# The bonus of eight chunks summed on TensorE instead of GpSimd, with the opening put in another order

## The chip, the core and the metric
The kernel runs on one core of one Trainium2 chip. The metric is the time of one execution on the device in microseconds (us), the median of several runs; lower is better. PE is TensorE, DVE is VectorE, ACT is ScalarE, POOL is GpSimd, and SP is the engine that issues the loads.

## What is computed
A recurrence over 768 time steps for 4 batches of 8 heads of 48 elements, and a gated feed-forward network (FFN) on its output.

```
for t in range(768):                                     # per batch and head
    y[t]  = r[t] @ (state + outer(u * k[t], v[t]))       # u * k: the "bonus" of the step itself
    state = w[t][:, None] * state + outer(k[t], v[t])
x = y as 3072 rows of 384 = 8 * 48
out = (sigmoid(x @ w_gate) * (x @ w_val)) @ w_out        # 384 -> 1536 -> 384
```

The bonus part of y[t] is the number sum(r[t] * u * k[t]) of each head, times v[t].

## The kernel before, in words
The steps are cut into 24 chunks of 128 (6 along time for each of 4 batches; c0 to c3 are the first chunks of the four batches, c4 to c7 the second). Of each chunk two tensors are loaded. `pin` holds decay, k and r "in lanes": 112 partitions (two heads of 48 at 0 and 64), four pairs of heads along the free axis. `tok` holds r, k and v "in rows": 128 time steps by 3 x 384. A chunk passes through

- `prep_k`, `prep_r` (DVE): two scans over the decay (L320, L337), k and r multiplied by them (L326, L342);
- `turn_k` (PE, four transposes, L352), `take_k` (ACT copy), `sums` (PE), `middle` and `keep` (the state after half a chunk and at its end);
- `scores` (PE), `mask` (DVE, two), `mix` (PE), `take_y` (DVE, two: adds the bonus), `turn_x` (PE), `take_x` and `rest_x` (ACT and DVE split x into a high and a low part);
- the bonus: `bonus1`, `bonus2` (POOL: r*u, then *k, in rows), `bonus3` (DVE: sum over each head, L309), `bonus4` (POOL: times v, L313).

The FFN's 12 weights w0 to w11 come as 64-bit floats, 1152 KB each. DVE rebuilds 32-bit floats from the words in three instructions (L250, L254, L258), ACT rounds off a high part (L263), DVE subtracts the low part (L266). ACT also checks each weight's range (`w_guard`). One FFN unit is one weight for one group of rows: `gate` and `value` on PE (pg and pu, nine matmuls each, L450), sigmoid, product, high and low part on ACT and DVE (sg, hm, hh, hl; L461 to L476), and `down` on PE (po, three matmuls a chunk, L485).

The first two rounds of four chunks (n = 0, 1) are cut into two groups of two chunks each. Their units, the chunks c0 to c12 and the weights are put in order at build time by `Plan`: each step has an engine, a guessed cost, the steps that it needs, the buffers that it takes and gives (`ROOM`), and a rank. `TURNS` gives the rank of chunks and weights, `COMES` the order of the loads on SP (strictly in order), `LAGS` how far the four FFN groups are set back. The later rounds are written out in a fixed loop. Each engine then works through its instructions in order; SP too, so a load that waits for a buffer holds all loads behind it. `pin` and `tok` have two buffers each.

Of the kernel before, what the change touches and what calls it, by code (L numbers as in the profile page):

```python
# [32 lines left out]
TURNS = "c0 w0 c1 w1 c2 w2 w3 w4 w5 c3 w6 w7 w8 c4 w9 w10 w11 c5 c6 c7 c8 c9 c10 c11 c12"  # L33
COMES = "p0 t0 ub w0 p1 p2 t1 w1 w2 p3 t2 t3 w3 w4 w5 t4 p4 w6 w7 w8 w9 w10 w11 p5 t5 t6 p6 t7 p7 p8 t8 t9 p9 p10 p11 t10 t11 p12 p13 t12 t13"
GROUPS = [(0, 0, 2), (0, 2, 4), (1, 0, 2), (1, 2, 4)]
LAGS = [0, 6.5, 15, 16]
ROOM = dict(pin=2, tok=2, bon=2, eg=1, ready=2, mid=2, kT=1, at=1, bank=2, x=2, full=1, pg=1, pu=1, unit=4, po0=1, po1=1, po2=1, po3=1)
HC = C // 2
HALVES = [slice(0, HC), slice(HC, C)]
HW = 3 * DM // 2  # L40
# [100 lines left out]
class Plan:  # L141
# [5 lines left out]
    def add(self, name, engine, cost, after, rank, work=None, take=(), give=()):  # L147
        self.ops[name] = (engine, cost, [a for a in after if a], rank, work, take, give)

    def run(self):  # L150
        left = {n: set(o[2]) for n, o in self.ops.items()}
        room, free, ends, order, started = self.room, {}, [(0.0, "")], [], set()
        transfers = [n for n in sorted(self.ops, key=lambda n: self.ops[n][3]) if self.ops[n][0] == "SP"]
        while ends:
            now = min(ends)[0]
            for e in [e for e in ends if e[0] <= now]:
                ends.remove(e)
                if e[1] in self.ops:
                    for r in self.ops[e[1]][6]:
                        room[r] += 1  # L160
                    for n in left:
                        left[n].discard(e[1])
            moved = True
            while moved:
                moved = False
                for n in sorted((n for n in self.ops if n not in started and not left[n]), key=lambda n: self.ops[n][3]):
                    engine, cost, _, _, work, take, _ = self.ops[n]
                    if engine and free.get(engine, 0.0) > now or engine == "SP" and n != transfers[0]:
                        continue
                    if any(room[r] < take.count(r) for r in take):  # L170
                        continue
                    for r in take:
                        room[r] -= 1
                    if engine:
# [7 lines left out]
                    if work:  # L182
                        work()
# [477 lines left out]
```

## Time and profile before

| what | us |
|---|---|
| median of 3 runs | 620.96 (620.81 to 621.43) |
| the profiled execution's own time | 622.11 |
| its span in the profile | 620.4 |
| PE busy | 577.6 |
| DVE, ACT, POOL busy | 334.7, 201.5, 96.6 |

The profile lists for one execution what each engine did and when, and what ended each idle time. Busy time of PE counts slow matmuls too: the granted clock says how fast PE was allowed to run, 1.00 at 2.4 GHz, 0.50 at 1.2 GHz. Of a stretch, the difference between its length and PE's busy time is time in which PE stood.

### The profile page before, as it was taken

What the parts mean: (1) busy time and instruction counts of PE and PEld (TensorE: products, weight loads), DVE (VectorE), ACT (ScalarE), POOL (GpSimd) and SP (SyncE); (2) the same over time, 40 slices, a digit from 0 to 9 for tenths busy, and PEclk for the clock granted to TensorE, in tenths of its full rate; (3) what the DMA queues carried; (4) which work ended last, traced back from release to release, by engine and by line L of the source; (5) the groups of instructions that cost most, each with busy time, mean ns of one, the idle gap of its engine ahead of it and who ended that gap; (6) DMA issues with size and microseconds to landing.
All of it is one profiled execution on the core that took longest, in us unless ns stands there. A gap on an engine that the chain in (4) does not pass through costs nothing. (4 is left out here: it accounts for less than half of the span.)

```text
span 620.4 us, 13068 instructions
## 1 busy us (share of the span) xinstructions
PE 577.6 (93%) x5706; PEld 513.6 (83%) x5706; DVE 334.7 (54%) x570; ACT 201.5 (32%) x402; POOL 96.6 (16%) x86
## 2 busy tenths in 40 slices
PE   4477799999999999799999999999999999999994
PEld 3376699999999999688888888888888888888884
DVE  4979879989575743234544544644644544212120
ACT  2638783444323322212312322312322312221112
POOL 3342111111121402002202202202202201000000
PEclk9998899999999999989999999999999999999999
DMA  8687920023223130121022042022042000000001
GB/s 247 232 323 275 348 85 1 2 84 109 76 82 124 46 123 1 52 84 50 35 84 53 33 134 66 18 84 69 17 135 84 1 1 2 25 28 0 1 2 55
DMA packets 12050, 50.76 MB, mean 82 GB/s; under 512 B 1376, under 2 KB 4576, under 8 KB 10448
## 3 DMA queue, kind: packets, MB, share of 16 engines
q1 hardware_dynamic: 8528, 45.11, 22.2%
q10 hardware_dynamic: 3456, 4.72, 2.1%
q8 instruction: 47, 0.77, 0.5%
q14 instruction: 19, 0.16, 0.1%
HBM read 45.11 MB, written 4.72 MB: 80 GB/s over the span
## 5 line engine op out<-in xcount | busy, mean ns | idle before, releaser
L450 PE MATMUL pg<-x,w 128*128 128x256 f32 (+1 forms) x864 | 173.9, 347 | 1.2 <-DVE w L266 1.2
L450 PE MATMUL pu<-x,w 128*128 128x256 f32 (+1 forms) x864 | 171.4, 344 | 0.0
L450 PEld LDWEIGHTS pg<-x,w 128*128 128x128 f32 x864 | 137.9, 193 | 18.0 <-DVE w L266 1.6
L450 PEld LDWEIGHTS pu<-x,w 128*128 128x128 f32 x864 | 136.7, 192 | 17.2
L485 PE MATMUL po<-w,hh 128*128 128x384 f32 x576 | 147.8, 338 | 0.0
L468 DVE TENSOR_TENSOR sg<-pu,sg 128x256 f32<-128x256 f32 (+1 forms) x96 | 53.4, 556 | 151.2 <-PE pu L450 150.1
L485 PE MATMUL po<-w,hl 128*128 128x384 f32 x288 | 101.6, 353 | 7.2 <-DVE hl L476 7.0
L485 PEld LDWEIGHTS po<-w,hh 128*128 128x128 f32 x576 | 105.2, 189 | 0.9
L472 ACT CAST hh<-sg 128x256 fp32r<-128x256 f32 (+1 forms) x96 | 49.1, 512 | 168.9 <-DVE sg L468 168.4
L461 ACT ACTIVATE sg<-pg 128x256 f32<-128x256 f32 (+1 forms) x96 | 46.9, 488 | 158.9 <-PE pg L450 158.1
L313 POOL TENSOR_TENSOR bon<-tok,a 128x384 f32<-128x384 f32 x24 | 35.2, 1465 | 296.9 <-DVE a L309 296.9
L476 DVE TENSOR_TENSOR hl<-sg,hh 128x256 fp32r<-128x256 f32 (+1 forms) x96 | 55.1, 574 | 38.8 <-ACT hh L472 38.8
L485 PEld LDWEIGHTS po<-w,hl 128*128 128x128 f32 x288 | 54.4, 189 | 10.7 <-DVE hl L476 8.7
L302 POOL TENSOR_TENSOR bon<-tok,ub 128x384 f32<-128x384 f32 x24 | 31.9, 1330 | 117.5 <-DMA tok<-tok 51.1
L424 DVE TENSOR_TENSOR bon<-pa,bon 128x192 f32<-128x192 f32 x48 | 15.6, 352 | 42.3 <-PE pa L417 42.3
L347 ACT ACTIVATE junk<-eg 112x1032 bf16<-112x1032 f32 x24 | 25.6, 1066 | 31.2 <-DVE eg L337 31.1
L417 PEld LDWEIGHTS pa<-tok,at 64*64 64x64 f32 x768 | 26.7, 143 | 9.1 <-issue 5.1
L320 DVE TENSOR_TENSOR_SCAN eg<-pin,ends 112x516 f32<-112x516 f32 x24 | 30.0, 1249 | 4.2 <-DMA pin<-dec 4.2
L417 PE MATMUL pa<-tok,at 64*64 64x48 f32 x768 | 29.9, 229 | 2.3 <-DVE at L383 2.3
L383 DVE TENSOR_TENSOR at<-pa,after 128x256 f32<-128x256 f32 x48 | 18.6, 418 | 24.7 <-PE pa L377 24.7
L337 DVE TENSOR_TENSOR_SCAN eg<-pin,heads 112x516 f32<-112x516 f32 x24 | 31.0, 1292 | 0.0
L395 PEld LDWEIGHTS pv<-tok,kT 64*48 64x48 f32 (+1 forms) x704 | 21.0, 137 | 10.7 <-issue 4.7
(58 smaller groups left out, 445.1 us busy)
## 6 DMA issues: line engine op xcount, KB each, us to landing
pin<-dec SPq DMA_DIRECT2D x23, 675.5 KB, 5.1
tok<-tok SPq DMA_DIRECT2D x24, 576.0 KB, 4.3
wraw<-wts SPq DMA_DIRECT2D x12, 1152.0 KB, 12.1
y<-o ACTq DMA_DIRECT2D x24, 192.0 KB, 2.1
pin<-dec SPq DMA_DIRECT2D x1, 448.0 KB, 4.1
pin<-dec SPq DMA_DIRECT2D x1, 227.5 KB, 2.6
ub<-u SPq DMA_DIRECT2D x1, 192.0 KB, 7.4
```

The source lines that it names most:

```text
L302: nc.gpsimd.tensor_tensor(out=bon[q], in0=tk[q][:, 0:DM], in1=ub, op=ALU.mult)
L313: nc.gpsimd.tensor_tensor(out=by_head(bon[q]), in0=by_head(tk[q][:, 2 * DM:]), in1=a0, op=ALU.mult)
L320: nc.vector.tensor_tensor_scan(out=e[:, 516:0:-1], data0=t[:, 516:0:-1], data1=ends[:, 516:0:-1], initial=0.0, op0=ALU.mult, op1=ALU.add,)
L337: nc.vector.tensor_tensor_scan(out=e[:, WW:WW + 516], data0=t[:, 0:516], data1=heads[:, 0:516], initial=0.0, op0=ALU.mult, op1=ALU.add,)
L347: nc.scalar.activation(junk, both, AF.Square, accum_out=acc_d[:, q:q + 1])
L417: nc.tensor.matmul(bank["y", q, o][half, p], lhsT=att[q][half, o, p], rhs=values(q, p, o, half), start=q < B and not s and p == 0, stop=p ...
L450: nc.tensor.matmul(t, lhsT=w[f][:, cols], rhs=x[n][:, a, k, i0 * C:i1 * C], start=k == 0 and j == 0, stop=k == NKT - 1 and j == 2)
L461: nc.scalar.activation(sg, hid["g", n, f, i0], AF.Sigmoid)
L468: nc.vector.tensor_tensor(out=sg, in0=hid["u", n, f, i0], in1=sg, op=ALU.mult)
L472: nc.scalar.copy(hh, hid["s", n, f, i0])
L476: nc.vector.tensor_tensor(out=hl, in0=hid["s", n, f, i0], in1=hid["hi", n, f, i0].bitcast(F32), op=ALU.subtract)
L485: nc.tensor.matmul(po[n, i][:, :DM], lhsT=h[:, c], rhs=w[f][:, 2 * DM:], start=f == 0 and j == 0, stop=f == NFF - 1 and j == 2,)
```

## The change
For the first eight chunks (`FAST`) the bonus takes another way. DVE multiplies r by k in lanes (`product`, before prep_k overwrites k). In `turn_k` four more matmuls, one per pair of heads, take that product as weights and two columns of u (`ul`, zero outside its head) as the moving operand: the sums of the eight heads land behind the transposes, in the same bank, and ACT copies them to `a0`. POOL is left with `bonus4`; `tok` of these chunks loads v only. `ul` is cleared by POOL and loaded by two loads of single elements. `ub`, which only later chunks need, is loaded later.

Beside that: `w_guard` writes its unused result in bf16 to a buffer shared with `guard`; the last four outputs have a buffer each and are copied by ACT and DVE in turn, stored from ACT and SP; the planner's search is rewritten with a heap; costs of PE steps in the first round are set higher; and `TURNS`, `COMES` and `LAGS` are new.

```diff
-COMES = "p0 t0 ub w0 p1 p2 t1 w1 w2 p3 t2 t3 w3 w4 w5 t4 p4 w6 ...
-LAGS = [0, 6.5, 15, 16]
+COMES = "p0 ul t0 p1 w0 p2 t1 w1 t2 w2 p3 t3 w3 w4 w5 w6 p4 w7 t4 ...
+LAGS = [0, 1.5, 19, 14]
...
+FAST = 8
...
     def load_tok(q):
-        nc.sync.dma_start(tk[q], tok[place(q)])
+        first = 2 * DM if q < FAST else 0
+        nc.sync.dma_start(tk[q][:, first:], tok[place(q)][:, first:])
...
+    def load_u():
+        for o in range(2):
+            nc.sync.dma_start(ul[64 * o:64 * o + D, :, o], u.rearrange("(p o d) -> o d p", o=2, d=D)[o])
+    def product(q):
+        rk[q] = p1.tile([L, NP, C], F32, tag="rk", name=f"rk{q}")
+        nc.vector.tensor_tensor(out=rk[q], in0=rr(q), in1=kk(q), op=ALU.mult)
...
     def turn_k(q):
...
+        if q < FAST:
+            for p in range(NP):
+                nc.tensor.matmul(t[:, NP * L + 2 * p:NP * L + 2 * p + 2], lhsT=rk[q][:, p], rhs=ul[:, p], start=True, stop=True)
...
     def take_k(q):
...
+        if q < FAST:
+            bank["a0", q] = p2.tile([P, H], F32, tag="a0", name=f"a0{q}")
+            nc.scalar.copy(bank["a0", q], bank["k", q][:, NP * L:NP * L + H])
...
+    def send(n, i):
+        final = n == NC_ - 1
+        o = p2.tile([P, DM], F32, tag=("o", "tok", "pin", "bon")[i] if final else "o", name=f"o{n}_{i}")
+        rows = out[place(n * B + i) * C:(place(n * B + i) + 1) * C, :]
+        if final and i % 2:
+            nc.vector.tensor_copy(o, po[n, i][:, :DM])
+            nc.sync.dma_start(rows, o)
+        else:
+            nc.scalar.copy(o, po[n, i][:, :DM])
+            nc.scalar.dma_start(rows, o)
```

The order on SP at the start, before (the number behind a name is that of the buffer's use; pin, tok and wraw come in the order of their chunks and weights):

```order
L277 DMA pin_103<-dec 112x520
L278 DMA pin_103<-dec 112x1024
L285 DMA tok_106<-tok 128x1152
L514 DMA ub<-u 128x384
L237 DMA wraw_113<-wts 128x1152
L280 DMA pin_179<-dec 112x1544
L280 DMA pin_205<-dec 112x1544
L285 DMA tok_210<-tok 128x1152
L237 DMA wraw_226<-wts 128x1152
L237 DMA wraw_261<-wts 128x1152
L280 DMA pin_303<-dec 112x1544
```

and now:

```order
L288 DMA pin_105<-dec 112x520
L289 DMA pin_105<-dec 112x1024
L314 DMA ul<-u 48x4x1 x2
L297 DMA tok_110<-tok 128x384
L291 DMA pin_112<-dec 112x1544
L248 DMA wraw_120<-wts 128x1152
L291 DMA pin_219<-dec 112x1544
L297 DMA tok_242<-tok 128x384
L248 DMA wraw_244<-wts 128x1152
L297 DMA tok_262<-tok 128x384
L248 DMA wraw_285<-wts 128x1152
L291 DMA pin_350<-dec 112x1544
```

The load of ul stands ahead of tok0, pin1 ahead of w0; tok of chunk 2 has come between w1 and w2.

On DVE, the stretch up to the second x, which the first FFN unit needs, before (pin_205 is chunk 2, w_220 and w_341 are w0 and w1):

```order
L424 TENSOR_TENSOR bon_229<-pa_1_270,bon_229 128x4x48
L337 SCALAR_TENSOR_TENSOR eg_329<-pin_205,heads 112x516
L342 TENSOR_TENSOR pin_205<-pin_205,eg_329 112x512
L442 TENSOR_TENSOR x_217<-px_345,x_217 128x3x128
L266 TENSOR_TENSOR w_341<-full_296,w_341 128x1152
```

and now (full_347 and w_355 belong to w2, pin_350 is chunk 3):

```order
L265 SCALAR_TENSOR_TENSOR full_347<-wraw_285,full_347 128x1152
L412 TENSOR_TENSOR at_318<-pa_0_319,after 128x256
L269 SCALAR_TENSOR_TENSOR full_347<-wraw_285,full_347 128x1152
L412 TENSOR_TENSOR at_318<-pa_1_320,after 128x256
L277 TENSOR_TENSOR w_355<-full_347,w_355 128x1152
L453 TENSOR_TENSOR bon_250<-pa_0_319,bon_250 128x4x48
L319 TENSOR_TENSOR rk_377<-pin_350 112x512
L453 TENSOR_TENSOR bon_250<-pa_1_320,bon_250 128x4x48
L343 SCALAR_TENSOR_TENSOR eg_382<-pin_350,ends 112x516
L347 RECIPROCAL heads<-eg_382 112x4
L349 TENSOR_TENSOR pin_350<-pin_350,eg_382 112x512
L471 TENSOR_TENSOR x_260<-px_386,x_260 128x3x128
```

Three weights, w0, w1 and w2, are now finished ahead of the second x, where before only w0 was; the k part of chunk 3 has come ahead of it too.

On PE, the end of the planned part (the second round's last units, then the first unit of the fixed loop), before:

```order
L450 MATMUL pg_2_11_3113<-x_1026,w_1586 128x256 x9
L485 MATMUL po_2_2198<-w_1462,hl_2_10_3123 128x384
L485 MATMUL po_2_2198<-w_1462,hh_2_10_3111 128x384 x2
L485 MATMUL po_3_2202<-w_1462,hl_2_10_3123 128x384
L485 MATMUL po_3_2202<-w_1462,hh_2_10_3111 128x384 x2
L450 MATMUL pu_2_11_3133<-x_1026,w_1586 128x256 x9
L485 MATMUL po_2_2198<-w_1586,hl_2_11_3146 128x384
```

and now:

```order
L479 MATMUL pg_0_11_3147<-x_1113,w_1594 128x256 x9
L479 MATMUL pu_0_11_3163<-x_1113,w_1594 128x256 x9
L514 MATMUL po_0_2077<-w_1355,hl_0_10_3159 128x384
L514 MATMUL po_0_2077<-w_1355,hh_0_10_3157 128x384 x2
L514 MATMUL po_1_2081<-w_1355,hl_0_10_3159 128x384
L514 MATMUL po_1_2081<-w_1355,hh_0_10_3157 128x384 x2
L514 MATMUL po_0_2077<-w_1594,hl_0_11_3182 128x384
```

The first group of the round, not the second, now ends last, and the down step of unit 10 stands between the last value and its own down step.

## Rows read from the trace of the kernel before
**Rows 1.** The page, busy tenths of PE in 40 equal slices of the span.
```profile
PE   4477799999999999799999999999999999999994
```
**Rows 2.** Stretches: length, busy of PE, PEld, DVE, ACT, POOL (instructions), clock, DMA share, GB/s.
```profile
0.00:44.00 44.00, 23.15 (x301) 20.09 (x304) 30.07 (x41) 19.77 (x33) 17.62 (x25) 1.00 0.80 282
44.00:84.00 40.00, 32.76 (x440) 29.78 (x436) 35.88 (x55) 31.96 (x58) 7.16 (x6) 0.87 0.66 244
84.00:248.00 164.00, 162.60 (x1952) 156.04 (x1951) 118.15 (x214) 58.98 (x136) 28.82 (x24) 1.00 0.23 69
...
52.00:72.00 20.00, 14.71 (x168) 12.95 (x165) 18.13 (x27) 15.17 (x29) 3.31 (x3) 0.74 1.01 406
260.00:272.00 12.00, 10.24 (x144) 8.20 (x140) 3.32 (x8) 1.22 (x2) 0.00 (x0) 0.72 0.27 72
```
**Rows 3.** PE in order of time: start us, us, what it did.
```profile
39.59 2.29 PE L450 MATMUL pg<-x,w 128*128 128x256 f32 x9
...
89.65 1.24 PE L450 MATMUL pu<-x,w 128*128 128x256 f32 x9
90.73 0.34 PE L485 MATMUL po<-w,hl 128*128 128x384 f32 x1
...
91.78 0.49 PE L429 MATMUL px<-ident,bon 128*128 128x128 f32 x3
```
**Rows 4.** DVE in order of time, idle time before in brackets.
```profile
3.55 1.23 DVE L320 TENSOR_TENSOR_SCAN eg<-pin,ends 112x516 f32<-112x516 f32 x1 [3.55 <-DMA pin<-dec]
...
5.34 0.69 DVE L326 TENSOR_TENSOR pin<-pin,eg 112x512 f32<-112x512 f32 x1 [0.27 <-DMA pin<-dec]
...
14.77 0.76 DVE L250 TENSOR_SCALAR full<-wraw 128x1152 int32<-128x1152 int32 x1 [1.74 <-DMA wraw<-wts]
...
17.24 1.35 DVE L258 SCALAR_TENSOR_TENSOR full<-wraw,full 128x1152 int32<-128x1152 int32 x1
...
22.67 2.03 DVE L337 TENSOR_TENSOR_SCAN eg<-pin,heads 112x516 f32<-112x516 f32 x1
...
26.23 0.54 DVE L309 TENSOR_REDUCE a<-bon 128x8 f32<-128x384 f32 x1
...
83.71 1.35 DVE L266 TENSOR_TENSOR w<-full,w 128x1152 fp32r<-128x1152 f32 x1
```
**Rows 5.** What DVE waited for up to 110 us: total, times, longest.
```profile
DVE sg L468 <- PE pu L450: 7.4, 6, 2.4
...
DVE a L309 <- POOL bon L305: 1.7, 1, 1.7
```
**Rows 6.** SP's issues and POOL in order of time.
```profile
3.13 9.37 SPq L280 DMA_DIRECT2D pin<-dec  x2
...
3.21 0.18 POOL L226 MEMSET fine<- 128x96 f32 x1
```
**Rows 7.** The page's DMA issues: count, KB each, median us to landing.
```profile
ub<-u SPq DMA_DIRECT2D x1, 192.0 KB, 7.4
```
**Rows 8.** PE in order of time: four transposes, and the sums of one chunk.
```profile
51.76 0.55 PE L352 MATMUL pk<-ident,pin 112*128 112x112 f32 x4
...
77.56 0.94 PE L395 MATMUL pv<-tok,kT 64*64 64x48 f32 x32
```
**Rows 9.** PE in order of time, where it stood around the plan's end.
```profile
250.10 0.44 PE L485 MATMUL po<-w,hl 128*128 128x384 f32 x1 [1.20 <-DVE hl L476]
...
253.96 0.45 PE L485 MATMUL po<-w,hl 128*128 128x384 f32 x1 [1.48 <-DVE hl L476]
...
262.32 1.48 PE L370 MATMUL pa<-pin 48*64 48x64 f32 x29 [1.62 <-DVE mid L406]
```
**Rows 10.** All engines in order of time at the very end.
```profile
611.89 0.51 PE L485 MATMUL po<-w,hh 128*128 128x384 f32 x2
...
614.25 0.48 ACT L491 COPY o<-po 128x384 f32<-128x384 f32 x1 [1.95 <-SPq L628]
...
615.82 0.34 ACTq L493 DMA_DIRECT2D y<-o  x1
```

More of the change, by code (lines that the diff above doesn't have):

```diff
@@ L1 @@
+import heapq
 from contextlib import ExitStack
@@ L147, in add @@
     def add(self, name, engine, cost, after, rank, work=None, take=(), give=()):
-        self.ops[name] = (engine, cost, [a for a in after if a], rank, work, take, give)
+        self.ops[name] = (engine, cost, {a for a in after if a}, rank, work, take, give)
     def run(self):
[L151 to L162, printed above, removed]
+        room, left, users, ready = self.room, {}, {}, {}
+        for n, o in self.ops.items():
+            left[n] = len(o[2])
+            for a in o[2]:
+                users.setdefault(a, []).append(n)
+        transfers = sorted((n for n, o in self.ops.items() if o[0] == "SP"), key=lambda n: self.ops[n][3])
+        for n in (n for n in self.ops if not left[n]):
+            ready.setdefault(self.ops[n][0], []).append(n)
+        free, events, order = {}, [(0.0, "")], []
+        while events:
+            now = events[0][0]
+            while events and events[0][0] <= now:
+                done = heapq.heappop(events)[1]
+                for r in self.ops[done][6] if done else ():
+                    room[r] += 1
+                for n in users.get(done, ()):
+                    left[n] -= 1
+                    if not left[n]:
+                        ready.setdefault(self.ops[n][0], []).append(n)
             moved = True
@@ L220, in tile_kernel @@
     ub = const.tile([P, DM], F32, name="ub")
+    ul = const.tile([L, NP, 2], F32, name="ul")
+    nc.gpsimd.memset(ul, 0.0)
     acc_d = const.tile([L, NG], F32, name="acc_d")
@@ L489, in down @@
             if f == NFF - 1:
-                o = p2.tile([P, DM], F32, tag="o", name=f"o{n}_{i}")
-                nc.scalar.copy(o, po[n, i][:, :DM])
-                g = place(n * B + i)
-                nc.scalar.dma_start(out[g * C:(g + 1) * C, :], o)
+                send(n, i)
+    def send(n, i):
[8 more added lines that the diff above has]
+            nc.scalar.dma_start(rows, o)
     def check_bounds():
@@ L545, in tile_kernel @@
         first = q % B == 0
-        add(f"tx{q}", "PE", 0.33, [f"y1{q}", q % B and f"tx{q - 1}"], k + 0.4, turn_x, q, take=["bank"] + ["x"] * first, give=["bon"])
+        add(f"tx{q}", "PE", 0.4 * slow, [f"y1{q}", q % B and f"tx{q - 1}"], k + 0.4, turn_x, q, take=["bank"] + ["x"] * first, give=["bon"])
         add(f"xh{q}", "ACT", 0.68, [f"tx{q}"], k, take_x, q)
```

82 lines of the change are left out of this document (45 added, 37 removed).

## The prediction
> **What bounds the kernel now.** I read the busy slices first: TensorE (PE) stands at 4 to 7 tenths in the first five slices of 15.5 us and near full behind them [rows 1]. The stretches say the same in numbers [rows 2]: from 0 to 84 us PE works 55.91 of 84 us, from 84 to 248 it works 162.60 of 164. So a microsecond is won where PE gets its first work earlier, at the two stretches where the clock is down (0.74 and 0.72 of full), and behind the last matmul. VectorE (DVE) paces the front: it is busy 65.95 of the 84 us, since every weight takes four of its instructions. There the rows show PE at two speeds: nine matmuls of 256 columns took 2.29 us at 39.59, and follow each other 1.08 us apart from 89 us on; a down step of six takes 1.05 us [rows 3]. The granted clock reads 1.00 in the first case too, so before the first record the matmul's duration tells the level (1.2 against 2.4 GHz).
>
> **The opening.** I compare the two kernels at the same amount of work done, and let DVE set when the changed one is there. Before, at 84 us: chunks 0 to 3 done, chunk 4 up to its scores, units 0 to 4 of the first FFN group and half of two units of the second, w0 to w4 split and w5 one instruction short. For the changed kernel I take the point where w6 and the split of chunk 3's x are done on DVE, since both pg 0_6 and the second group's first unit can then start, and all of the order behind it finds its weights ready.
>
> DVE's work to that point is 65.95 us [rows 2] plus the differences, from rows [rows 4]: the last step of w5, 1.35 less 0.29 already counted (+1.06); all of w6, 0.75 and three times 1.35 (+4.8); five products r*k, which have the shape of L326 (0.69 us, so +3.45); five reduces gone (0.54 each, -2.7); of chunk 4 no mid, state and masks yet (-1.46). In the other direction, DVE instructions run long while GpSimd (POOL) runs: a scan took 2.03 us at 22.67 one of the same size 1.23 at 3.55 [rows 4]. Eight such rows before 84 us add 4.4 us. POOL's busy time there is 24.8 us, 2.5 of it memsets [rows 2]; the change leaves five multiplies of about 1.2 us, a quarter to a third, so -2.9. Sum: 68.2 us.
>
> It starts later: the product needs the second half of pin0, which landed at 5.34 [rows 4], where the first scan needed only the first half. What remains are DVE's waits. Before, counted from its first instruction at 3.55, they were 84 - 3.55 - 65.95 = 14.5 us: 7.4 us up to 110 us for value matmuls, 1.7 for the reduce's input, 1.74 for w0 [rows 4, 5], and smaller ones. In the new order I follow the chain by hand with these durations: w0 still lands near 15 us and DVE gets to it at 12.5 (wait 2.5 to 3); mix 0 at PE's slow speed (0.5); two splits wait for ScalarE's cast (0.8 to 1 each); w3 can be issued only behind tok3, which waits for mix 1 near 40.6 (0.7); hidden steps (0.5). That is 6.3 us, as each weight is finished two or three steps ahead of its unit instead of one. So 5.3 + 68.2 + 6.3 = **79.8 us**. By then PE has done 14 up steps and 6 down steps against 13 and 5, but not the scores of chunk 4: 1.08 + 1.05 - 1.1 = +1.0 us of work. Gain: 84.0 + 1.0 - 79.8 = 5.2. The first FFN matmul comes later, near 44 us instead of 39.59, but with three weights ready. I take off 1.7 us for POOL's multiplies, whose hits on DVE fall where DVE is the pace: **-3.5 us**. Bounds: if DVE waits 14.5 us as before, the point moves to 88.0, and with those hits the change loses 4.7 here; if it waits only for w0 (2.5 us) and the hits fall elsewhere, it gains 9.
>
> Loads: eight chunks load 192 KB instead of 576. I price that at nothing by itself: the weights are in time once issued, and what held them was SP, which stood 9.37 us over two pin issues until chunk 0's scores [rows 6]. In the new order pin2 still stands there, now behind the transposes of chunk 1 as well, some 4 us later; the shorter tok loads and w0 put behind pin1 pay that back. New on SP is the load of ul (two issues): it waits for POOL's memset of that tile, next to the one at 3.21 [rows 6], so tok0, pin1 and w0 are issued near 4.3 to 5.7 instead of 1.7 to 3.5. w0 was not late because of its issue but because of the bytes ahead of it, so I charge 0 to 2 us, inside the bounds.
>
> The ul load moves 384 single elements of 4 bytes. No row shows such a load: the nearest is ub, 7.4 us from issue to landing, behind tok0 [rows 7]. Issued near 3.5, ul would by that be there at 10.9, and turn_k of chunk 0 could run from 8.1; as chunk 0 has slack until w0 lands, even that hides. The Trainium skill, "DMA: Bandwidth & Descriptors" (Rules for kernel authors), speaks against it: a last dimension that is not contiguous becomes one descriptor per element. Its measured table (Bandwidth) gives about 10.5 ns a packet, by which 384 packets would be an estimated 4 us of the queue in front of tok0, pin1 and w0, and the sum would be 4 us worse.
>
> **TensorE's new matmuls.** 32 of them, two columns wide with 128 columns of r*k as weights. Those of chunks 0 to 3 fall where PE waits. Those of chunks 4 to 7 lengthen PE, 16 of them. Below: 32 small matmuls of the sums take 0.94 us, 0.03 each; four transposes with the same size of weights take 0.55, 0.14 each [rows 8]. The weights have the transposes' size, so I take 0.13: **+2.1 us**. Bounds 0.5 and 4.3 (twice the transposes' share, since these are true f32 products). The extra small copy on ScalarE and POOL's multiply are hidden by the same wait for the masks; if not, 0.3 us a chunk.
>
> **The plan's end.** Before, the last two down steps of the second group wait 1.20 and 1.48 us for hl [rows 9]: ScalarE copies out first, then up and down of one unit follow each other with nothing between. The new lags let the first group end last, with down 0_10 between up 0_11 and its own down: 1.05 us of work in the 1.48 us gap, and no copies in front. About 0.5 us stays: **-2.2 us** (-1 to -2.7).
>
> **The clock.** Behind that end the granted clock falls: 0.72 over 260 to 272 is 12 x 0.28 x 2 = 6.7 us at 1.2 GHz, so 3.4 us of work given away [rows 2]. Ahead of it PE stood three times in 14 us [rows 9]; the third (1.62 us, for mid) stays. With one long stand instead of three I expect no fall: **-3.4 us**; 0 if it falls. The same at 52 to 72 us (10.4 us at half speed) I have taken as gone above, since PE now waits for less than 4 us between 44 and 80.
>
> **The tail.** The last matmul ends at 612.4; the third output copy waits for a free o buffer until 614.25, the fourth behind it, and the last store is issued at 615.82 [rows 10]. With four buffers and two copying engines the last copy (0.5 us) starts at 612.5 and is issued on SP by 613.1: **-2.8 us** (-2.3 to -3.1).
>
> **Sum.** -3.5 + 2.1 - 2.2 - 3.4 - 2.8 = -9.8 us. On the profiled execution's own 622.11 that is 612.3; it lies 1.15 over the median of the runs shown, 620.96, so against that **611.2 us**.
>
> **Rivals.**
> 1. The clock falls once more, either behind the plan's end or near 60 us, because one stand is enough. For it: the stand of 1.62 us stays [rows 9]. Against: between 44 and 84 us PE stood 7.2 of 40 us [rows 2], now less than 4. +3.4: **614.6** (25%).
> 2. The ul load holds the queue as long as ub's row shows: issued near 3.9 and landed 7.4 later [rows 7], 11.3; behind it tok0, pin1 and w0, 2.05 MB at the stretch's 282 GB/s [rows 2], 7.3 us: w0 at 18.6 instead of near 15, DVE standing in front of it. +3.8: **615.0** (10%). That is what the page named above would bring about; no row bears it out or excludes it.
> 3. Slower: SP stands at tok3 (free only after mix 1), and w3 to w6 stand behind it. If mix 1 ends near 40 us, w3 lands at 47 and DVE hardly waits. Decisive is 52 us: from there on each microsecond delays every weight behind. With mix 1 at 52, w3 lands at 58: DVE and PE lose 11 us, the clock falls again (3.4 more), and 611.2 + 11 + 3.4 = **625.6**. Against it: mix 1 needs of DVE only the masks behind two weights, and the chain above has 11 us to spare. 4%.
> 4. The change works, but moves no bound: the saving on POOL and DMA is off the path, DVE waits as before in another place (-3.5 becomes +4.7), tail and end win the rest: **619.4** (7%).
>
> **How the numbers follow.** My forecast 54%, with opening gains up to 8 us inside it; its own range is 606.5 to 614. The rivals have 25, 10, 4 and 7. A range of 606 to 617.5 holds forecast, rivals 1 and 2, and leaves out 4, 3 and the better end. A measurement here can tell 0.2%, 1.24 us: faster is all but rival 3, some of 4 and their sums with 1 or 2: 0.93; same 0.02; slower 0.05.
>
> **What would show it.** Right: w6 split by about 77 us on DVE and PE nearly gapless from 80; DVE's waits before that about half of 14.5 us; granted clock at 1.00 between 50 and 72 and behind the plan's end; the last store under 1.5 us behind the last matmul; the new matmuls near 0.5 us a chunk. Wrong: the first DMA-bound wait of DVE behind w3 longer than 3 us; turn_k of chunk 0 waiting for ul past 11 us; a granted clock of 0.50 anywhere after 50 us.

## The result and the profile after

The changed kernel is slower: 622.92 us (median of 20 runs, 619.69 to 624.91) against 620.33 (20 runs beside them), ratio 1.0036, 95% interval 1.0019 to 1.0052. Forecast were 611.2 us and a range of 606 to 617.5. The profiled execution took 623.8 us, with a span of 622.1; before, 622.11 and 620.4.

The stretches of the changed kernel, with the columns of [rows 2] (busy of PE, PEld, DVE, ACT, POOL, then granted clock, DMA share, GB/s):

```profile
0.00:44.00 44.00, 21.80 (x265) 19.70 (x266) 32.91 (x43) 18.40 (x32) 5.75 (x18) 1.00 0.49 162
44.00:84.00 40.00, 38.41 (x450) 35.51 (x449) 36.24 (x54) 30.44 (x59) 2.33 (x2) 1.00 0.69 256
84.00:248.00 164.00, 162.16 (x2020) 155.75 (x2016) 112.41 (x212) 62.48 (x144) 20.81 (x20) 1.00 0.27 81
52.00:72.00 20.00, 19.30 (x225) 18.29 (x225) 17.56 (x27) 18.73 (x36) 1.50 (x1) 1.00 0.69 238
260.00:272.00 12.00, 10.24 (x145) 8.21 (x145) 3.38 (x8) 1.21 (x2) 0.00 (x0) 0.72 0.25 66
```

Much looks as forecast: the granted clock no longer falls between 52 and 72 us (0.74 before [rows 2]), PE works 38.41 of 40 us from 44 to 84, POOL is down from 17.62 to 5.75 us in the first stretch. Yet the work is not done earlier. A good mark is the late loop's first gate matmul, where the plan ends: 255.11 us before, 255.36 now. From there to the last matmul's end, in instructions that the change does not touch, it is 357.29 us before (255.11 to 612.40) and 359.24 now (255.36 to 614.60); behind that, 8.0 and 7.5 us to the end of the span. So +0.25, +1.95 and -0.5, which is the 1.7 between the spans. The mark of one trace is good to about a microsecond only: nine traces of the changed kernel and of versions with the same plan have it between 254.75 and 256.06 (255.4 on the average), three of the kernel before at 252.03, 254.78 and 255.11.

Part of the 38.41 us is slow work, which the clock column does not show, as no level is recorded that early. Nine matmuls of 256 columns take 2.29 us at half speed and follow each other some 1.1 us apart at full speed [rows 3]. In the kernel before they are fast from 44.99 us on, here only from 54.96:

```profile
44.99 1.34 PE L450 MATMUL pg<-x,w 128*128 128x256 f32 x9
```

```profile
47.04 2.29 PE L479 MATMUL pg<-x,w 128*128 128x256 f32 x9
...
51.15 2.29 PE L479 MATMUL pu<-x,w 128*128 128x256 f32 x9
53.23 1.89 PE L479 MATMUL pg<-x,w 128*128 128x256 f32 x9
54.96 1.22 PE L479 MATMUL pu<-x,w 128*128 128x256 f32 x9
```

What PE did with the new matmuls, in order of time (four matmuls leave eight records, x8): in the opening, at the slow speed, 1.66 us pass from their start at 14.82 to the next instruction, later 0.82 (from 59.78).

```profile
14.82 1.73 PE L378 MATMUL pk<-ul,rk 112*128 112x2 f32 x8
16.48 0.47 PE L399 MATMUL pa<-pin 48*64 48x64 f32 x2
...
59.78 0.96 PE L378 MATMUL pk<-ul,rk 112*128 112x2 f32 x8
60.60 0.53 PE L458 MATMUL px<-ident,bon 128*128 128x128 f32 x3
```

What DVE waited for from its first instruction to 83 us (total, times, longest; the 7.2 of the first row holds the 4.90 before its start):

```profile
DVE rk L319 <- DMA pin<-dec: 7.2, 3, 4.9
DVE w L277 <- ACT w L274: 2.9, 4, 0.9
DVE at L412 <- PE pa L406: 1.1, 1, 1.1
DVE sg L497 <- PE pu L479: 1.0, 2, 0.6
DVE x L471 <- ACT x L467: 0.9, 1, 0.9
DVE eg L343 <- ACT junk L370: 0.9, 1, 0.9
DVE bon L453 <- PE pa L446: 0.2, 1, 0.2
```

PE's stands around the plan's end, to be held against [rows 9]. The wait for hl at 250.10 and its 1.20 us are now at 241.86, the last one is 0.44; the wait for mid in front of the late loop's first scores is still 1.62, and behind it the clock is down again (0.50 from 263 to 269):

```profile
254.21 0.44 PE L514 MATMUL po<-w,hl 128*128 128x384 f32 x1 [0.44 <-DVE hl L505]
...
262.59 1.48 PE L399 MATMUL pa<-pin 48*64 48x64 f32 x29 [1.62 <-DVE mid L435]
```

One fact about the runs is needed for what follows: this last fall is in most runs of the changed kernel, not in all. Of twelve traces of the changed kernel and its versions with this stand, four have the fall as long as here, five half as long, three not at all. Of the 20 timed runs 13 have a mean clock of 0.994 or below (the one shown has 0.991), with spans some 3 us longer than the other seven.

### The profile page after: what moved, and what is told of

Read it like the earlier page. It is cut to its first block, busy times and chain, and to the rows that moved or that the text cites. A ratio compares the mean times of both kernels' runs of the same rounds, so it can differ in the third digit from the quotient of the medians.

```text
span 622.1 us, 13174 instructions
## 1 busy us (share of the span) xinstructions
PE 585.9 (94%) x5770; PEld 521.2 (84%) x5770; DVE 333.7 (54%) x572; ACT 201.1 (32%) x408; POOL 71.8 (12%) x71
## 4 chain that ended last, share of the span: by engine, by line
PE 86%; DVE 6%; ACT 3%; DMA 2%; issue 1%; SPq 0%; ACTq 0%; DVEq 0%
PE pg L479 24%; PE pu L479 24%; PE po L514 23%; PE pa L446 4%; PE pv L424 3%; PE pa L399 2%; PE pa L406 2%; PE pk L375 1%; DMA pin<-dec 1%; PE px L458 1%; DMA wraw<-wts 1%; PE pk L378 1%; DVE w L277 1%; DVE hl L505 1%; ACT sq L255 1%
## 5 line engine op out<-in xcount | busy, mean ns | idle before, releaser
L336 POOL TENSOR_TENSOR bon<-tok,a 128x384 f32<-128x384 f32 x24 | 32.0, 1334 | 388.3 <-DVE a L330 273.4
L323 POOL TENSOR_TENSOR bon<-tok,ub 128x384 f32<-128x384 f32 x16 | 21.4, 1338 | 52.5 <-DMA tok<-tok 45.7
```

The costliest lines, as they stand in the source:

```text
L336: nc.gpsimd.tensor_tensor(out=by_head(bon[q]), in0=by_head(tk[q][:, 2 * DM:]), in1=a0, op=ALU.mult)
```

## The experiments

**The stand before the scores.** The first unit of the late loop is put in another order: transposes before its gate, sums before its value matmuls.

```diff
+                first = not last and n == 2
+                if first:
+                    trio[i][0]()
                 gate(*a)
                 sigmoid(*a)
-                trio[i][0]()
+                if first:
+                    trio[i][1]()
+                else:
+                    trio[i][0]()
                 value(*a)
...
-                trio[i][1]()
+                if not first:
+                    trio[i][1]()
```

> The changed kernel with one reordering in the first unit of the late loop: transposes of k in front of the gate, the sums in front of the value matmuls, so that mid is there when the scores come. The stand of 1.62 us in front of the scores (261 to 262.6) should go. Theory: that one stand is what the granted clock falls behind (0.50 from 263 to 269), so both go: 1.6 + 3.4 = 5.0 us, span 617.1. Rival: the clock falls at that place whatever stands in front of it (a 0.44 us wait for hl at 254 stays): 1.6 us only, span 620.5, granted clock 0.50 somewhere in 255 to 275.

618.76 us, ratio to the kernel before 0.9965 (0.9947 to 0.9982). The stand is gone and no clock fall is left; none of its 12 runs has a mean clock under 0.997. The stretches of this run:

```profile
248.00:260.00 12.00, 11.56 (x99) 10.19 (x98) 2.42 (x6) 3.67 (x8) 0.00 (x0) 1.00 0.10 34
260.00:272.00 12.00, 12.00 (x143) 9.95 (x142) 6.26 (x12) 2.32 (x5) 0.00 (x0) 1.00 0.33 108
```

From the first late gate matmul to the last matmul it takes 353.67 us, 5.57 less than the changed kernel, where 5.0 was expected. So the one stand of 1.62 us is what this fall stands behind, even where the 0.44 us wait at 254 remains. The stand alone is worth more than its 1.62 us: the version with the old tail (below) has the stand and no fall, and takes 355.92, 2.25 us more. The same edit in the kernel before:

> The kernel before, with nothing of the change, but the late loop's first unit reordered. The stand of 1.62 us in front of the scores goes, and the fall of the clock behind it, which in the kernel before is in a quarter of the runs. Theory: 1.6 to 2.4 us less: 618.0 to 618.8, ratio 0.996 to 0.997, and the changed kernel with the same reordering (0.9965) is no better than this, so that the change itself, without its tail, is worth nothing. Rival: the changed kernel's opening leaves a gain of over 1 us once the late loop is the same: then this stays above 619.5.

617.77 us, 0.9949 (0.9930 to 0.9967): 0.2 us under the forecast's lower end, and its late loop is 352.09 us instead of 357.29. With the same late start the changed kernel (0.9965) is no better than the kernel before: the change itself won nothing. Its plan ends no earlier (255.33 against 254.78 us), and its late loop has a loss of its own, which the last group of experiments takes up.

**The bonus matmuls.** Each issued twice:

```diff
-            for p in range(NP):
+            for p in [p for p in range(NP) for _ in range(2)]:
                 nc.tensor.matmul(t[:, NP * L + 2 * p:NP * L + 2 * p + 2], lhsT=rk[q][:, p], ...
```

> The changed kernel with each of the 32 small bonus matmuls issued twice (the second writes the same again). It doubles their cost and nothing else. In the trace of the changed kernel four of them take 0.82 us at 2.4 GHz and 1.66 at 1.2 GHz. Mark: the late loop's first gate matmul (255.4). Theory: each costs what its row shows, and those of the chunks 0 to 3, at the slow clock, are on the path as well: 4 x 1.66 + 4 x 0.82 = 9.9 us at most, and I take 6 to 9: 261.5 to 264.5. The prediction's price of 0.13 us each with only those of chunks 4 to 7 on the path: 2.1 us, 257.5. Rival: they run in gaps of PE: below 1 us.

The mark moves from 255.36 to 263.34: 7.98 us for 32 matmuls, 0.25 each, inside the theory's range. The price of 0.13 with nothing for the first chunks falls, and so does the rival. Then the price from below, first with one record a matmul instead of two:

```diff
+    ulr = const.tile([L, NP, 2], F32R, name="ulr")
...
-        rk[q] = p1.tile([L, NP, C], F32, tag="rk", name=f"rk{q}")
+        rk[q] = p1.tile([L, NP, C], F32R, tag="rk", name=f"rk{q}")
...
+            if q == 0:
+                nc.scalar.copy(ulr, ul)
...
-... lhsT=rk[q][:, p], rhs=ul[:, p], ...
+... lhsT=rk[q][:, p], rhs=ulr[:, p], ...
```

> The changed kernel with r*k and u in the fp32r format for the 32 small bonus matmuls, which so take one pass over their weights instead of two; products are then rounded, the bonus is less exact. One small copy on ScalarE is added. Theory: each of the four costs half, 0.41 us a chunk at 2.4 GHz and 0.8 at 1.2 GHz; the late loop's first gate matmul comes 3 to 4.5 us earlier than 255.4. By the prediction's price (0.13 each, half of it gained): 1.0 us. Rival: the time of such a matmul is the load of its 128 columns of weights, which one pass does not shorten: within 0.5.

Four matmuls take 0.45 us instead of 0.82 (0.92 at the slow clock instead of 1.66), but the mark comes only 0.95 us earlier, at 254.41. That is little more than the spread of single traces. The run stood 2.9 us earlier at the last chunk's bonus matmuls (137.63 against 140.54); a new wait of 1.59 us for hl at 153.74 and a few small ones took most of it back. And with one matmul a chunk:

```diff
-            for p in range(NP):
-                nc.tensor.matmul(t[:, NP * L + 2 * p:NP * L + 2 * p + 2], lhsT=rk[q][:, p], rhs=ul[:, p], ...
+            nc.tensor.matmul(t[:, NP * L:NP * L + H], lhsT=rk[q][:, 0], rhs=ul.rearrange("a p o -> a (p o)"), ...
```

> The changed kernel with one bonus matmul a chunk, eight columns wide, instead of four of two columns; three quarters of the products r*k are left out of the bonus. Mark: the late loop's first gate matmul, 255.4. Doubling them cost 8.0 us, halving their passes gave 0.95. Theory: their price is the same both ways and the one-pass run lost its gain to a new wait for hl of its own at 153.7 us: 4 to 6 us earlier, 249.4 to 251.4. Rival: below the present cost other engines set the pace, VectorE's hidden values above all: 1 to 2.5 us earlier and the rest in waits for hl.

The mark is at 251.81, 3.55 us earlier: between theory and rival, with no wait for hl beyond those of the changed kernel (1.20, 0.44 and one of 0.27). So the matmuls cost the path 3.55 us or more as they are, and each further microsecond of them costs about one (doubling adds 3 x 1.66 + 5 x 0.82 = 9.1 us of PE's time and moves the mark by 7.98); not all of the 8 us can be had back. The marks of the two runs, PE in order of time:

```profile
263.34 2.25 PE L479 MATMUL pg<-x,w 128*128 128x512 f32 x9
```

```profile
251.81 2.25 PE L478 MATMUL pg<-x,w 128*128 128x512 f32 x9
```

Is the new way still better than the old one for chunks 4 to 7?

```diff
-FAST = 8
+FAST = 4
-... p4 w7 t4 w8 t5 w9 w10 w11 p5 p6 t6 t7 p7 p8 ub t8 ...
+... p4 w7 ub t4 w8 t5 w9 w10 w11 p5 p6 t6 t7 p7 p8 t8 ...
```

> The changed kernel with the new bonus only for the chunks 0 to 3; chunks 4 to 7 load r, k and v in rows again and form the bonus on GpSimd and VectorE as before, the load of u moved ahead of tok4. The planner finds its order with the same tables. Theory: TensorE is the bound from 80 us on, so leaving out 16 small matmuls there saves 4 x 0.82 = 3.3 us: the late loop's first gate matmul at 252.1 instead of 255.4. Rival: GpSimd's three multiplies a chunk slow VectorE again, and its reduce waits for them: 255 to 258, with TensorE's waits between 84 and 250 above 2 us.

The mark is later, 257.48: the rival's side. The granted clock from 44 to 84 us is 0.91, PE is busy 35.36 of these 40 us instead of 38.41, and x of chunk 3 starts its last split at 87.14 instead of 82.87. With the tables of eight chunks the old bonus for four of them costs 2.1 us, though it saves 3.3 on PE. In that run the clock falls at the end of a stand of 2.35 us for hl (at 71.8), and 0.09 x 40 = 3.6 us of work are given away by the fall; what the old bonus would cost without it this run does not tell.

**SyncE's stand at pin2.** A third pin buffer, the order of instructions unchanged:

```diff
+    p3 = own.enter_context(tc.tile_pool(name="p3", bufs=3))
...
-        t = p2.tile([L, WW + 2 * NP * C], F32, tag="pin", name=f"pin{q}")
+        t = p3.tile([L, WW + 2 * NP * C], F32, tag="pin", name=f"pin{q}")
...
-        o = p2.tile([P, DM], F32, tag=("o", "tok", "pin", "bon")[i] if final else "o", name=f"o{n}_{i}")
+        o = p2.tile([P, DM], F32, tag=("o", "tok", "x", "bon")[i] if final else "o", name=f"o{n}_{i}")
```

> The changed kernel with three buffers for the lanes (pin) instead of two, in the same order of instructions. SyncE need not stand until the scores of chunk 0 before it issues pin2 (19.27 us), nor w1, tok2, w2 and pin3 behind it. Theory: VectorE's waits in the opening, which the prediction put at 6.3 us and which were 9.96, are 1.41 for pin2 and what follows from its lateness: x of chunk 3 ends 2 to 3.5 us earlier than 83.4. Rival: pin2 merely hides a wait for the mixes and for ScalarE's casts; VectorE waits at the next place and x of chunk 3 is less than 1 us earlier. Second rival: the earlier transfers take bandwidth from w0 and delay it: later than before.

SP's issues of pin in the changed kernel (pin1 and pin2, then the next):

```profile
4.69 0.43 SPq L291 DMA_DIRECT2D pin<-dec  x1
...
19.27 0.32 SPq L291 DMA_DIRECT2D pin<-dec  x1
...
36.75 0.33 SPq L291 DMA_DIRECT2D pin<-dec  x1
```

and with three buffers:

```profile
4.70 0.43 SPq L292 DMA_DIRECT2D pin<-dec  x1
5.64 0.43 SPq L292 DMA_DIRECT2D pin<-dec  x1
```

x of chunk 3 starts its last split 1.39 us earlier (81.48 against 82.87) and the mark comes 1.05 us earlier, at 254.31. The 1.39 lie between the theory's 2 to 3.5 and the rival's 1: in this trace pin2's lateness costs what its wait shows (1.41 us), and little behind it. Three later versions with three pin buffers (below) end their plan earlier still, at 252.53 to 253.37 us; with this one they average 253.2, which is 2.2 us before the 255.4 of two buffers.

**The tail.** The old tail in the changed kernel:

```diff
-        final = n == NC_ - 1
+        final = False
```

> The changed kernel with the old tail: all four last outputs copied by ScalarE into two buffers and stored from its queue. The prediction's tail term says that this costs 2.8 us (622.1 to 624.9 of span). Theory from the trace of the changed kernel: the new tail gains only 0.5, as the span ends 7.5 us behind the last matmul against 8.0 before, so about 8.0 again: 622.6. The trace tells it: time from the last matmul's end to the end of the span, 8.0 by both; 7.5 in the changed kernel.

7.98 us from the last matmul to the end, as in the kernel before (8.0). Time: ratio 1.0050 (1.0030 to 1.0069), too near the changed kernel's 1.0036 to be told from it. The stores from ScalarE's queue:

```diff
             nc.vector.tensor_copy(o, po[n, i][:, :DM])
-            nc.sync.dma_start(rows, o)
         else:
             nc.scalar.copy(o, po[n, i][:, :DM])
-            nc.scalar.dma_start(rows, o)
+        nc.scalar.dma_start(rows, o)
```

> The changed kernel, but the last outputs 1 and 3, which VectorE copies, are stored from ScalarE's queue instead of SyncE's. Theory: in the changed kernel SyncE reads the flag for the last branch only behind its stores, and that ends the program 6.2 us after the last store was issued; before, with the flag read long ago, the program ended 4.2 us after it. Then the end comes about 2 us earlier: 5.5 us behind the last matmul instead of 7.5, span 620.1, ratio to the changed kernel 0.997. Rival: the end is set by the last store's own landing and by the engines' meeting at the end, whatever queue issued it: 7.5 stays within 0.5.

7.16 us, the rival's side; ratio 1.0025 (1.0005 to 1.0045). It was no clean test, as ScalarE's queue now waited for VectorE's first copy (the issue at 612.63 took 1.82 us) and the third copy came late:

```profile
612.63 1.82 ACTq L529 DMA_DIRECT2D y<-o  x2
614.54 0.48 ACT L528 COPY o<-po 128x384 f32<-128x384 f32 x1 [1.94 <-DVE o L526]
615.05 0.82 ACTq L529 DMA_DIRECT2D y<-o  x2
```

Reading the flag ahead of the last unit, which is in four of the versions below, gave 5.93 to 6.39 us; the new tail without it 6.31 to 7.5 in eleven traces, 6.81 on the average. So the flag behind the stores is probably a part, about 0.7 us by the averages; the two groups overlap, and those versions have other edits too. The rest of what ends the program stays open.

**The late loop's units.** The gate matmuls of the last twelve units start at (first and twelfth of them) 533.95 and 603.53 before, 69.58 us, and in the changed kernel at

```profile
535.12 1.09 PE L479 MATMUL pg<-x,w 128*128 128x512 f32 x4
...
605.67 1.55 PE L479 MATMUL pg<-x,w 128*128 128x512 f32 x6
```

70.55 us, which is 11 units from start to start: 6.414 a unit instead of 6.325. Instructions and their order are the same there. The groups of PE from 545 to 600 us (count, busy us, mean ns) show the value matmuls at 389 ns before,

```profile
L450 PE MATMUL pg<-x,w 128*128 128x512 f32 x81 | 20.2, 393 | 0.0
L450 PE MATMUL pu<-x,w 128*128 128x512 f32 x78 | 19.3, 389 | 0.0
```

and at 395 after:

```profile
L479 PE MATMUL pu<-x,w 128*128 128x512 f32 x81 | 20.4, 395 | 0.0
L479 PE MATMUL pg<-x,w 128*128 128x512 f32 x75 | 18.9, 394 | 0.0
```

What the change can touch there is the places of tiles in memory: it adds ul ahead of the weights, and drops the weight guard's f32 tile, which lay between the weights and x. That tile put back:

```diff
-        sq = p1.tile([P, 3 * DM], BF16, tag="junk", name=f"sq{f}")
+        sq = p1.tile([P, 3 * DM], F32, tag="sq", name=f"sq{f}")
```

> The changed kernel with the old f32 tile of the weight guard (a tile of its own, 4.6 KB a partition) instead of the bf16 tile that it shares. It does the same work in the same order; only the places of tiles in memory and the type of one scratch tile differ. Theory: the places are what makes the late loop's units slower (the last twelve take 6.31 us each, 6.22 before; 1.95 us from the loop's first matmul to its last): 6.22 again and 2 us less, span 620.1. Rival: the late loop's speed varies from run to run, whatever the kernel: 6.2 to 6.3 in all four runs of this set without order. Second rival: the guard's type matters on ScalarE: its two passes take other times in the opening, some tenths of a us.

6.327 a unit, and 354.27 us for the late loop against 355.92 in the run with the old tail, both without a fall of the clock: 1.65 us. Ratio 0.9993 (0.9974 to 1.0011). Then only a place kept free, with no use:

```diff
+        if f == 0:
+            p1.tile([P, 3 * DM], F32, tag="sq", name="pad")
```

> The changed kernel with one tile of 4.6 KB a partition reserved where the old f32 tile of the weight guard lay, and never used; the guard stays in the shared bf16 tile. Theory: only the places of the tiles behind it count: the last twelve units take 6.33 us each as before the change (6.38 to 6.41 with the change), and the time falls to that of the run with the guard's own tile: ratio to the kernel before 0.999, about 2 us under the changed kernel. Rival: the guard's type or its sharing of a tile counts: 6.38 to 6.41 stays, ratio 1.003.

6.415: the rival's number, though for another reason, as the next runs show. Ratio 1.0029 (1.0013 to 1.0045). The pad of 4.6 KB had not put the tiles where the guard's tile does: by the allocator's addresses x begins 224 bytes further on, since the shared tile is longer. With 256 bytes, `[P, 64]` in place of `[P, 3 * DM]`:

> The changed kernel with an unused tile of 256 bytes a partition behind the shared bf16 tile, nothing else. In all kernels so far the tiles of x and of the hidden values (sg, hh, hl) begin at 192 or 224 modulo 512 bytes where the last twelve units take 6.325 to 6.328 us (the kernel before with and without the reordering, and both with the guard's own tile), and at 448 or 480, or x at 384, where they take 6.377 to 6.415 (the changed kernel and all others; the pad of 4.6 KB left them at 448). The 256 bytes move them to 192. Theory: that place is the cause: 6.33 us, ratio 0.999. Rival: the place is chance and the guard's f32 tile counts in another way: 6.38 to 6.41, ratio 1.003.

6.414, ratio 1.0034 (1.0013 to 1.0055): the rule of 512 bytes falls. With 32 bytes (`[P, 8]`):

> The changed kernel with an unused tile of 32 bytes a partition behind the shared bf16 tile, nothing else. The rule of 512 bytes fell. What still sorts all fourteen kernels is the place modulo 64 bytes of the weights against that of x and of the hidden tiles: equal (0 and 0, or 32 and 32) where the last twelve units take 6.325 to 6.328 us, unequal where they take 6.377 to 6.415. The change adds a tile of 32 bytes (ul) ahead of the weights, and takes the f32 guard tile from behind them. The 32 bytes put x at 32 like the weights. Theory: 6.33 us, from the late loop's first matmul to its last 1.6 us less, ratio to the kernel before 0.999 to 1.001. Rival: the sorting is chance: 6.38 to 6.41, ratio 1.003.

6.325 a unit, 354.26 us for the late loop; ratio 1.0012 (0.9991 to 1.0032). First and twelfth gate matmul of this run, 69.58 us apart as before the change:

```profile
531.12 1.09 PE L481 MATMUL pg<-x,w 128*128 128x512 f32 x4
...
600.70 1.55 PE L481 MATMUL pg<-x,w 128*128 128x512 f32 x6
```

and its groups from 545 to 600 us:

```profile
L481 PE MATMUL pg<-x,w 128*128 128x512 f32 x81 | 20.2, 393 | 0.0
L481 PE MATMUL pu<-x,w 128*128 128x512 f32 x81 | 19.8, 389 | 0.0
```

The same 32 bytes in the kernel before:

> The kernel before, with nothing of the change, but an unused tile of 32 bytes a partition in the pool behind the weights, so that x lies at 32 and the weights at 0 modulo 64. Theory: the late loop becomes as slow as that of the changed kernel: 6.38 to 6.41 us a unit instead of 6.325, ratio to the kernel before 1.0025. Rival: 6.325 stays, ratio 1.000.

6.390 a unit (530.52 to 600.81), value matmuls at 395 ns:

```profile
L452 PE MATMUL pu<-x,w 128*128 128x512 f32 x81 | 20.4, 395 | 0.0
L452 PE MATMUL pg<-x,w 128*128 128x512 f32 x79 | 19.8, 394 | 0.0
```

So 32 unused bytes make the loop faster in one kernel and slower in the other: the place is the cause. The time of the whole does not decide the second (1.0013, 0.9994 to 1.0031): the interval holds both the theory's 1.0025 and the rival's 1.000.

**Versions meant to beat both**, first with three repairs: the guard's own tile, the late start, and the flag read early, of which the last is new:

```diff
+    bad = nc.values_load(flag[:1, :1])
     down(*last.pop())
     own.close()
-    with tc.If(nc.values_load(flag[:1, :1]) != 0):
+    with tc.If(bad != 0):
```

> The changed kernel with three repairs at once: the weight guard's old f32 tile, the late loop's first unit reordered as in the run before, and the flag for the last branch read ahead of the last unit's output, so that SyncE no longer reads it behind its stores. Theory: the first two add up, as they lie in different places: from the late loop's first matmul to its last 353.67 - 1.65 = 352.0 us; the third lets the span end 5.5 us behind the last matmul instead of 6.5 to 7.5. Span 255.5 + 352.0 + 5.5 = 613.0, 614.7 by the program's own time, ratio to the kernel before 0.991. If the flag is not what ends the program, 6.9 instead of 5.5: 616.1.

616.39 us, 0.9929 (0.9910 to 0.9949). The late loop takes 351.99 us, as expected to the tenth: the two repairs add up. The flag gave less than hoped (6.39 us behind the last matmul). Against the kernel before with the late start alone (0.9949) the intervals overlap. Then with three pin buffers instead of the guard's tile, late start and early flag kept, and pads of 256 bytes, of 32, and of 32 with 32 more in each pin buffer:

> The version meant to beat both: the changed kernel with three pin buffers, the 256 bytes that put the late tiles at 224 modulo 512 (x at 128), the late loop's first unit reordered and the flag read early. Theory: the opening's 1.05 us of the run with three pin buffers adds to the run with three repairs (616.4): 615.3, ratio 0.991. If x has to begin at 192 or 224 as well: 1.5 us worse, 616.8.

616.95 us, 0.9949 (0.9932 to 0.9966); 6.391 a unit.

> The version meant to beat both: as d3_pin3_pad, but with a pad of 32 bytes: x at 32 like the weights, the hidden tiles at 0. Theory: it is x against the weights that counts, as TensorE's up matmuls were the slower ones: 6.33 us a unit, 1.6 us under d3_pin3_pad (616.95): 615.3, ratio 0.992. If the hidden tiles count too, between the two.

614.81 us, 0.9911 (0.9893 to 0.9928), the lowest of all, and the only interval that lies clear of that of the kernel before with the late start (0.9930 to 0.9967). But its units took 6.395, so what it has won over the version with 256 bytes did not come from the units: its plan ends at 252.72 us against 253.37.

> As d5_best, with 32 more bytes in each of the three pin buffers, so that the weights, x and the hidden tiles all lie at 32 modulo 64. With x alone equal to the weights (d5_best) a unit took 6.395 us, with the hidden tiles alone equal to them (the runs with three pin buffers before) 6.391 and 6.393. Theory: all three have to be equal: 6.33 us a unit, the late loop 1.2 to 1.6 us shorter than in d5_best (354.05), ratio to the kernel before 0.989. Rival: what counts lies elsewhere and three pin buffers are slower by themselves: 6.39 stays, ratio 0.991.

6.414 a unit, 615.83 us, 0.9930 (0.9908 to 0.9953). The rule of 64 bytes falls too. The places modulo 128 bytes, by the allocator's addresses:

```
kernel                                  weights   x   hidden  us a unit
before; with the late start                64    64     64    6.325; 6.327
change with the guard's own tile           96    96     96    6.327
the three repairs                          96    96     96    6.328
change + 32 bytes                          96    96     96    6.325
change; FAST = 4; + 4.6 KB; + 256 bytes    96    64     64    6.414 to 6.415
change with old tail; ScalarE's stores;
  bonus twice; late start; one a chunk     96    64     64    6.377 to 6.378
bonus in fp32r                              0    96     96    6.414
before + 32 bytes                          64    96     96    6.390
three pin buffers; + 256 bytes             96     0     96    6.393; 6.391
three pin buffers + 32 bytes               96    32      0    6.395
  and 32 more in each pin buffer           96    32     96    6.414
```

The fast kernels are those in which x lies like the weights modulo 128; the hidden tiles do so too in all five, so x alone need not be what counts. This rule was read off afterwards, and no run was made to test it. It also leaves something open: at the same places some versions took 6.378 a unit and some 6.414.

## Why the prediction was wrong

The sign was wrong: each term of the sum came out worse than forecast, and one came that was not in the sum.

**The opening (-3.5).** The step that failed is VectorE's waits: "That is 6.3 us", which were 9.96. DVE's work up to the split of x of chunk 3 was forecast at 68.2 us and is 68.55 (68.01 from 4.90 to 82.87 and the split's 0.54), its start at 5.3 and is 4.90; so the waits are 83.41 - 4.90 - 68.55 = 9.96. The point came at 83.4 and not at 79.8. w0, for which 2.5 to 3 us were set aside, cost nothing: it was there when DVE came to it at 14.13. Instead DVE waited 0.91 for pin1, 1.41 for pin2, 2.9 for ScalarE's casts (two at 0.8 to 1 were forecast), 0.9 for its guard, 1.1 for the scores of chunk 2. SP's stand at pin2, of which "the shorter tok loads and w0 put behind pin1 pay that back" was the forecast, cost 1.4 us there and 1.05 at the plan's end (third pin buffer; 2.2 on the average of four traces): pin2 was issued at 19.27 us, where it had been at 12.17, so 7 us later and not 4. The transposes with slow bonus matmuls ahead of the scores are in that stand. The two loads of ul, which were rival 2, each landed 1.9 us after their issue (3.34 and 3.7 us); the estimate of 4 us by the Trainium skill, "DMA: Bandwidth & Descriptors" (Bandwidth), is not borne out.

```profile
ul<-u SPq DMA_DIRECT2D x2, 0.8 KB, 1.9
```

**The new matmuls (+2.1).** Both factors failed. The price of 0.13 is 0.21 by the trace's 0.82 for four: each leaves two records, and with operands that leave one it took half (0.45 for four). And "Those of chunks 0 to 3 fall where PE waits" is wrong: chunk 3's stand at 59.78, where PE has no gap left; those of the first three lie ahead of the scores that SP waits for, and what they cost there was not measured by itself. Five times 0.82 is 4.1 us where PE is the bound, and with three quarters of the matmuls gone, the plan ends 3.55 us earlier.

**The plan's end (-2.2).** It gave -1.0: the waits are 1.20 + 0.44 us instead of 1.20 + 1.48. The step that failed is "About 0.5 us stays": the 1.20 did not go, it moved to 241.86.

These three were to give -3.6 us up to the mark at 255 and gave +0.25 in this pair of traces, so 3.85 us are missing. The point on DVE was 3.6 us late, but 1.7 of that had been taken off beforehand (for POOL's multiplies), which leaves 1.9; the matmuls make 2.0 more, the plan's end 1.2. That is 5.1, more than is missing, and the 1.25 us between are not explained (they are within the spread of the marks). Nor does DVE's point set PE's pace as the prediction has it: the point at x of chunk 3 is not what PE stood for, as it worked 38.4 of 40 us from 44 to 84 whatever DVE's mark.

A count of PE's work at one speed shows where the opening's gain went. It is an estimate in which busy time at half speed counts half: all of it up to 44 us (23.15 us before [rows 2], 21.80 now), and from there these stretches (length, busy of PE, granted clock, DMA share, GB/s), before

```profile
44.00:57.80 13.80, 11.02 (x167) 1.00 0.54 184
57.80:68.10 10.30, 8.46 (x76) 0.50 1.00 417
68.10:84.00 15.90, 13.27 (x201) 1.00 0.54 184
```

and now, where the first of the two is slow by the rows above:

```profile
44.00:54.60 10.60, 10.17 (x108) 1.00 1.00 411
54.60:84.00 29.40, 28.24 (x344) 1.00 0.58 200
```

So up to 84 us PE did 40.1 us of work before and 44.2 now. But 4.9 of the 44.2 are the new matmuls of six chunks at 0.82, and without them it is 39.3. The new order did win some 4 us for PE, about what was forecast, and the new matmuls used them up; of these six chunks the prediction charged only two, at 0.13 a matmul. That full speed came late is by itself hardly what took the gain: in six other versions it came some 3 us earlier, near 51, and they reach the mark at 254.75 to 255.74, hardly before these 255.36.

**The clock (-3.4).** It fell as before in the profiled run, and by their mean clock in most others, which was rival 1 (25%). "With one long stand instead of three I expect no fall" is the step that failed: one stand can be enough (nine of twelve traces), and without it there is none (0 of the 12 runs with the late start, nor in any run of the versions with it). Added to that, the prediction took the fall from one profiled execution of the kernel before and subtracted it from the median of all. The runs' mean clocks do not tell whether its median run had that fall, as they also hold the fall at 52 to 72. But the late start took only 2.8 us from that kernel's median (620.56 to 617.77), of which the stand itself is 2.25, if it is worth as much there as in the changed kernel: by this estimate the median run had little of the fall to give back. In the changed kernel the same edit took 4.2 us (622.92 to 618.76), so the fall is probably the more frequent there, which would be a part of why the medians lie 2.6 us apart and the two profiled spans 1.7.

**The tail (-2.8).** The copies end as forecast: the last one 0.60 us behind the last matmul (614.64 + 0.56 against 614.60), 3.39 before (615.31 + 0.48 against 612.40), so 2.8 earlier. But the end follows it after 6.9 us, not 4.6: the step that failed is that the end keeps its distance from the last copy. -0.5 in the profiled pair, -1.2 on the average of all traces. A part of it is probably the flag, read only behind SyncE's stores; the rest is open.

**What was not in the sum.** The late loop's units, +1.65 us from 32 bytes; the other 0.3 of its 1.95 us go with the 6.414 against 6.378 a unit, whose cause is open. The price of the edits in `ul` and `w_guard` was taken as that of their instructions alone.

Of the rivals, the first came true in its mechanism, though not in its time (614.6). The fourth (619.4) did not: with DVE waiting as before the mark would have come 4.7 + 2.1 - 2.2 = 4.6 us later, and it came 0.25 later. Rival 3, the only slower one, did not either: tok3 was issued at 42.26, w3 behind it, and no wait for it is in the trace. That the measured time is slower, as in rival 3, is no support for it.

## What to carry to other kernels

A gain on the pacing engine's work is not yet a gain: list the new order's waits one by one, and look at what each queue stands for (here SP at pin2), before anything is called hidden. Count an engine's busy time at one speed before you call it work done. A stand of a microsecond or two in front of the longest loop is worth more than it shows when the clock falls behind it; one reordering there gave about 3 us in the kernel before and 4 in the changed one. When untouched code gets slower, compare its instructions' mean ns and the addresses of its tiles, and try a pad, before blaming the run.

## What the runs showed of the hardware

- 32 bytes in the place of x and the hidden tiles change the matmuls of a loop that they bound: the value matmuls of 512 columns took 389 against 395 ns, the loop 354.3 against 355.9 us. Shown in both directions, in one trace of each kernel; the rule behind it is open.
- A true f32 matmul of two columns against 128 columns of weights took 0.205 us at the high clock and 0.415 at the low one; with fp32r operands 0.11 and 0.23.
- One stand of PE of 1.62 us was followed by a granted clock of 0.50 for some 7 us in one execution (0.72 over 260 to 272) and by 1.00 in another with the same stand, that of the 32-byte pad:

```profile
260.00:272.00 12.00, 10.24 (x162) 8.77 (x162) 4.82 (x11) 2.31 (x5) 0.00 (x0) 1.00 0.35 108
```
